# Own input buffers, an early fill and another row order for the last two supertiles of a pointwise convolution

## Chip, cores, metric

One core of a Trainium2 chip. The metric is the device time of one execution in microseconds (us), the median of several runs.

## The reference

```python
# x: (1, 384, 384, 384) bf16, dw: (1, 1, 384), pw: (384, 384)
out = xp[:, i:i+H, j:j+W, :] * dw[i, j]        # k = 1: one scale per channel
return jnp.einsum('bhwc,cd->bhwd', out, pw)
```

With k = 1 this is one matrix product: 147456 rows of 384 channels times a 384 x 384 matrix whose rows are scaled by dw. In and out are 113 MB each.

## The kernel before

Rows go in supertiles of 512, 288 in all. VectorE transposes a supertile, TensorE multiplies it, ScalarE copies the result from PSUM to an output buffer, SyncE issues loads and stores. Loads and stores are made for pieces of 1 to 10 supertiles, in three rotating buffers.

```python
LMAX = 10; NR = 3; LONG = 1
head, tail = [[1, 1, 2, 2, 4]], [[6, 4], [3, 2, 1, 1, 1]]   # between them 26 groups of [10]
...
def load_x(t, eng=nc.sync):
    g, i, off, first, L = chunks[t]
    dst = Xs[g % NR][:, 4 * off : 4 * (off + L), :]
    rows = xf[512 * first : 512 * (first + L), :]
    if first + LONG < NS:                       # all but the last supertile
        src = rows.rearrange("(p s) c -> p (s c)", p=P)        # one run of 3072*L bytes per partition
        ...
    else:                                       # the last supertile
        src = rows.rearrange("(a k q) c -> q a k c", k=4, q=4) # runs of 768 bytes
    ...                                         # waits until the buffer is free
    eng.dma_start(dst, src).then_inc(s_x[g % NR][i], 16)

def store(t):
    ...
    if first + LONG < NS:
        dst = rows.rearrange("(q p j) d -> p q (j d)", q=4, p=P)  # runs of 768*L bytes
    else:
        dst = rows.rearrange("(m q) d -> m (q d)", q=4)           # one run of 3072 bytes
    ...
```

The order of rows within a supertile is free, but the transposes tie input to output. With the plain order the input comes in runs of 3072 bytes and the output leaves in runs of 768; with the other order it is the reverse. Only the last supertile (287) used the other one. Its load was issued by ScalarE, at the copy of supertile 260, late in the run:

```python
for jj, (t, j) in enumerate(order):             # ScalarE's copies, in order
    ...
    a = nc.scalar.copy(Ov[:, 0:nq, j, :], PS[s][:, 0:nq, :D])
    ...
    if jj == g_end[len(groups) - 1 - NR] + 1:   # jj == 260
        for u in range(NT - LONG, NT):
            load_x(u, nc.scalar)
```

Of the kernel before, what the change touches and what calls it, by code (L numbers as in the profile page):

```python
# [7 lines left out]
BF16 = mybir.dt.bfloat16  # L8
F32 = mybir.dt.float32
U32 = mybir.dt.uint32  # L10
# [1 line left out]

LMAX = 10
NR = 3
LONG = 1


def _groups(n_super: int):

    head, tail = [[1, 1, 2, 2, 4]], [[6, 4], [3, 2, 1, 1, 1]]  # L20
    mid = n_super - sum(map(sum, head + tail))
    assert mid > 0 and mid % LMAX == 0
    return head + [[LMAX]] * (mid // LMAX) + tail
# [3 lines left out]
def kernel(  # L27
# [12 lines left out]
    nc = tc.nc  # L40
    P = nc.NUM_PARTITIONS
    B, H, W, C = x.shape
# [8 lines left out]

    NS = N // 512
    groups = _groups(NS)

    chunks, first = [], 0
# [4 lines left out]
    NT = len(chunks)  # L60
    g_end = [max(c[3] + c[4] for c in chunks if c[0] == g) - 1 for g in range(len(groups))]

    consts = ctx.enter_context(tc.tile_pool(name="consts", bufs=1))
    bufp = ctx.enter_context(tc.tile_pool(name="bufs", bufs=1))
# [11 lines left out]
    zero = consts.tile([P, D], BF16, name="zero")  # L76

    Xs = [bufp.tile([P, 4 * LMAX, C], BF16, name=f"X{i}") for i in range(NR)]
    Ts = [bufp.tile([P, NB, 256], BF16, name=f"T{i}") for i in range(2)]
    Os = [bufp.tile([P, 4 * LMAX * D], BF16, name=f"O{i}") for i in range(NR)]  # L80
    PS = [psum.tile([P, 4, 512], F32, name=f"ps{s}") for s in range(2)]

    s_x = [[nc.alloc_semaphore(f"s_x{i}{k}") for k in range(max(map(len, groups[i::NR])))] for i in range(NR)]
    s_t = [[nc.alloc_semaphore(f"s_t{i}{h}") for h in range(2)] for i in range(2)]
    s_pe = nc.alloc_semaphore("s_pe")
    s_a = [nc.alloc_semaphore(f"s_a{i}") for i in range(2)]
# [11 lines left out]
    s_zero = nc.alloc_semaphore("s_zero")  # L98

    with tc.tile_critical():  # L100
        def load_x(t, eng=nc.sync):
            g, i, off, first, L = chunks[t]
            dst = Xs[g % NR][:, 4 * off : 4 * (off + L), :]
            rows = xf[512 * first : 512 * (first + L), :]
            if first + LONG < NS:
                src = rows.rearrange("(p s) c -> p (s c)", p=P)
                dst = dst.rearrange("p s c -> p (s c)")
            else:
                src = rows.rearrange("(a k q) c -> q a k c", k=4, q=4)
            if g >= NR and (i == 0 or eng is not nc.sync):  # L110
                je = g_end[g - NR]
                eng.wait_ge(s_t[je % 2][1], je // 2 + 1)
            eng.dma_start(dst, src).then_inc(s_x[g % NR][i], 16)

        def store(t):
            g, i, off, first, L = chunks[t]
# [2 lines left out]
            rows = of[512 * first : 512 * (first + L), :]  # L119
            if first + LONG < NS:  # L120
                dst = rows.rearrange("(q p j) d -> p q (j d)", q=4, p=P)
# [8 lines left out]

        nc.scalar.dma_start(dw_row[:], dw.rearrange("a e c -> a (e c)")).then_inc(s_dw, 16)
        load_x(0, nc.scalar)
        nc.sync.dma_start(pw_n[:], pw.rearrange("(k p) d -> p k d", p=P)).then_inc(s_pw, 16)

        todo = []
        for t, (g, i, off, first, L) in enumerate(chunks):
            if 0 < t < NT - LONG:
                todo.append((g_end[g - NR] if g >= NR else -1, load_x, t))
            todo.append((first + L + 1, store, t))
# [109 lines left out]
        for s in range(2):  # L249
            c = nc.scalar.copy(warm[:, s + 1 : s + 2], warm[:, 0:1])  # L250
# [4 lines left out]
        def transposes(t, j):  # L255
            g, i, off, first, L = chunks[t]
            jj = first + j
            s = jj % 2
            Xw = Xs[g % NR][:].bitcast(U32)[:, 4 * off : 4 * (off + L), :].rearrange("p (k l) c -> p k l c", l=L)
            Tw = Ts[s][:].bitcast(U32).rearrange("p b (i k) -> p b k i", k=4)  # L260
            for h in range(2):
                if h == 0 and j == 0:
                    nc.vector.wait_ge(s_x[g % NR][i], 16 * sum(len(ls) > i for ls in groups[g % NR : g + 1 : NR]))
                ins = nc.vector.transpose(  # L264
                    out=Tw[:, 3 * h : 3 * h + 3],
                    in_=Xw[:, :, j, 96 * h : 96 * h + 96].rearrange("p k (b w) -> p b k w", w=32),
                )
                if jj >= 2:
                    ins._wait_ge(s_pe, 2 * (jj - 2) + h + 1)
                ins.then_inc(s_t[s][h])  # L270
# [24 lines left out]
        for i in range(6):  # L295
            w_out(i)
        transposes(*order[0])
        transposes(*order[1])

        for jj, (t, j) in enumerate(order):  # L300
            g, i, off, first, L = chunks[t]
            s = jj % 2
            Ov = Os[g % NR][:, 4 * off * D : 4 * (off + L) * D].rearrange("p (q j d) -> p q j d", q=4, d=D)
            if j == 0 and i == 0 and g >= NR:
                nc.scalar.wait_ge(s_o[g % NR], 16 * sum(map(len, groups[g % NR : g : NR])))
            nq = 4
            if jj + 1 == NS:
                nq = 2
                nc.vector.wait_ge(s_o[g % NR], 16 * sum(map(len, groups[g % NR : g : NR])))
                e = nc.vector.tensor_copy(Ov[:, nq:4, j, :], PS[s][:, nq:4, :D])  # L310
                e._wait_ge(s_pe, 2 * jj + 2)
                e.then_inc(s_d)
            a = nc.scalar.copy(Ov[:, 0:nq, j, :], PS[s][:, 0:nq, :D])  # L313
            a._wait_ge(s_pe, 2 * jj + 2)
            a.then_inc(s_a[s])
            if jj == g_end[len(groups) - 1 - NR] + 1:

                for u in range(NT - LONG, NT):
                    load_x(u, nc.scalar)
            if jj + 2 < NS:  # L320
                transposes(*order[jj + 2])

# [29 lines left out]
```

## Time and profile before

| before | |
|---|---|
| time, median of 3 runs | 575.55 us (575.28 to 575.68) |
| the profiled execution | 576.07 us, of which 574.3 us are the span in the profile |
| matmuls of the 288 supertiles | 561.8 us |
| last copy ends, last store issued, landed | 569.63, 569.72, 573.03 us |

The profiled execution was 0.5 us slower than the median.

### The profile page before, as it was taken

Reading aid. Unit: us, or ns where it says so; the run is one execution under the profiler, and the core shown is the slowest. Engines: PE = TensorE matmul, PEld = TensorE weight load, DVE = VectorE, ACT = ScalarE, POOL = GpSimd, SP = SyncE. Lnnn points to the kernel's source line nnn. Section 1 sums busy time; section 2 is a strip of 40 time slices with the busy share of each in tenths; the row PEclk is TensorE's granted clock in tenths of the full one; section 3 lists DMA queues with packets and bytes.
Section 4 is the critical chain, followed back from the end, with each engine's and each line's share of the span. In section 5 each row is a group of like instructions: output and inputs, shape, how many; then the busy total and the mean of one; then the engine's idle time right before and its main releaser. Section 6 shows DMA issues by size and latency. Waiting matters only on the chain.

```text
span 574.3 us, 29720 instructions
## 1 busy us (share of the span) xinstructions
PE 566.5 (99%) x13869; PEld 411.8 (72%) x13869; DVE 509.4 (89%) x583; ACT 418.7 (73%) x296; POOL 0.9 (0%) x8
## 2 busy tenths in 40 slices
PE   8999999999999999999999999999999999999996
PEld 5777777777777777777777777777777777777774
DVE  7899999999999999999999999999999999999994
ACT  6777777777777777777777777777777777777774
POOL 0000000000000000000000000000000000000000
PEclk9999999999999999999999999999999999999999
DMA  8999999999999999999999999999999999999776
GB/s 360 436 376 420 434 409 429 431 431 421 392 399 428 390 385 420 402 388 397 422 402 395 395 439 378 400 394 432 385 402 401 426 399 382 417 400 377 303 280 226
DMA packets 25936, 226.88 MB, mean 395 GB/s; under 512 B 1221, under 2 KB 5702, under 8 KB 22086
## 3 DMA queue, kind: packets, MB, share of 16 engines
q1 hardware_dynamic: 25264, 226.01, 97.6%
q10 hardware_dynamic: 662, 0.79, 0.4%
q14 instruction: 9, 0.07, 0.0%
q8 instruction: 1, 0.02, 0.0%
HBM read 113.54 MB, written 113.25 MB: 395 GB/s over the span
## 4 chain that ended last, share of the span: by engine, by line
PE 98%; ACT 0%; DVE 0%; issue 0%; POOL 0%; POOLq 0%; SPq 0%
PE ps L172 98%; PE ps L189 0%; ACT w_r L277 0%; DVE O L310 0%; PE ps L222 0%; POOL zero L238 0%; POOL warm L237 0%; PE ps L204 0%; POOLq L347 0%; SPq L100 0%
## 5 line engine op out<-in xcount | busy, mean ns | idle before, releaser
L172 PE MATMUL ps<-w_r,T 32*128 32x384 bf16 x13824 | 561.8, 321 | 0.7 <-ACT w_r L277 0.7
L264 DVE STREAM_TRANSPOSE T<-X 128x384 uint32<-128x384 uint32 x576 | 506.3, 881 | 53.7 <-DMA X<-in_x_dram 0.5
L313 ACT CAST O<-ps 128x1536 bf16<-128x1536 f32 x288 | 413.6, 1436 | 147.8 <-PE ps L172 147.8
L172 PEld LDWEIGHTS ps<-w_r,T 32*128 32x128 bf16 x13824 | 410.1, 93 | 152.2 <-issue 0.9
L277 ACT CAST w_r<-ps 128x768 bf16<-128x768 f32 x5 | 3.6, 820 | 1.0 <-PE ps L222 1.0
L189 PE MATMUL ps<-zero 32*128 32x384 bf16 x24 | 2.6, 494 | 1.4 <-POOL zero L238 1.4
L310 DVE CAST O<-ps 128x768 bf16<-128x768 f32 x1 | 1.0, 958 | 3.0 <-PE ps L172 3.0
L250 ACT ACT_TABLE_LOAD x1 | 1.3, 1283 | 1.9 <-issue 1.9
L189 PEld LDWEIGHTS ps<-zero 32*128 32x128 bf16 x24 | 0.7, 99 | 2.6 <-issue 2.6
L222 PE MATMUL ps<-pw_n,sel_w 64*128 64x384 bf16 x18 | 2.2, 395 | 0.0
L282 DVE TENSOR_REDUCE sel<-eye 128x64 f32<-128x128 bf16 x1 | 0.3, 290 | 1.8 <-POOL eye L240 1.8
L222 PEld LDWEIGHTS ps<-pw_n,sel_w 64*128 64x128 bf16 x18 | 0.9, 115 | 1.4 <-issue 0.7
L277 DVE CAST w_r<-ps 128x768 bf16<-128x768 f32 x1 | 1.0, 958 | 0.9 <-PE ps L222 0.9
L292 DVE TENSOR_SCALAR sel_w<-sel,dw_f 128x256 bf16<-128x256 f32 x3 | 0.9, 351 | 0.0
L289 DVE COPY dw_f<-ps 128x3 f32<-128x3 f32 x1 | 0.2, 160 | 0.8 <-PE ps L204 0.8
L204 PEld LDWEIGHTS ps<-ones,dw_row 1*128 1x128 bf16 x3 | 0.2, 102 | 0.2 <-issue 0.2
L240 POOL TENSOR_SCALAR_AFFINE_SELECT eye<-ones 128x128 bf16<-128x128 bf16 x1 | 0.3, 292 | 0.1
L250 ACT COPY warm<-warm 128x1 f32<-128x1 f32 x2 | 0.3, 189 | 0.0
L238 POOL MEMSET zero<- 128x192 uint32 x1 | 0.3, 258 | 0.0
L204 PE MATMUL ps<-ones,dw_row 1*128 1x1 bf16 x3 | 0.2, 162 | 0.0
L239 POOL MEMSET ones<- 128x128 bf16 x1 | 0.2, 204 | 0.0
L336 POOL MEMSET const-bfloat16-1.0<- 128x1 bf16 x1 | 0.1, 102 | 0.0
(4 smaller groups left out, 0.4 us busy)
## 6 DMA issues: line engine op xcount, KB each, us to landing
X<-in_x_dram SPq DMA_DIRECT2D x26, 3840.0 KB, 21.4
out_dram<-O SPq DMA_DIRECT2D x26, 3840.0 KB, 27.6
X<-in_x_dram SPq DMA_DIRECT2D x2, 1536.0 KB, 17.8
out_dram<-O SPq DMA_DIRECT2D x2, 1536.0 KB, 14.5
X<-in_x_dram SPq DMA_DIRECT2D x3, 768.0 KB, 7.1
out_dram<-O SPq DMA_DIRECT2D x3, 768.0 KB, 10.8
X<-in_x_dram SPq DMA_DIRECT2D x1, 2304.0 KB, 20.5
out_dram<-O SPq DMA_DIRECT2D x1, 2304.0 KB, 13.0
```

The lines of the kernel that those rows point to most:

```text
L172: mm = nc.tensor.matmul(PS[s][:, q, :D], lhsT=Ts[s][32 * q : 32 * q + 32, b, par::2], rhs=w_r[32 * q : 32 * q + 32, b, par, :], start=(b, ...
L189: nc.tensor.matmul(PS[0][:, i, :D], lhsT=zero[32 * i : 32 * i + 32, 0:P], rhs=zero[32 * i : 32 * i + 32, :], start=True, stop=True, tile_p ...
L204: mm = nc.tensor.matmul(PS[1][:, 0, D + k : D + k + 1], lhsT=dw_row[:, P * k : P * k + P], rhs=ones[0:1, 0:1], start=True, stop=True,)
L222: mm = nc.tensor.matmul(PS[(k + 1) % 2][:, 2 * r + v, :D], lhsT=sel_w[64 * v : 64 * v + 64, k, r, :, :].rearrange("p q w -> p (q w)"), rhs ...
L238: nc.gpsimd.memset(zero[:].bitcast(U32), 0).then_inc(s_zero)
L240: nc.gpsimd.affine_select(out=eye[:], in_=ones[:], pattern=[[-1, P]], compare_op=mybir.AluOpType.is_equal, fill=0.0, base=0, channel_multi ...
L250: c = nc.scalar.copy(warm[:, s + 1 : s + 2], warm[:, 0:1])
L264: ins = nc.vector.transpose(out=Tw[:, 3 * h : 3 * h + 3], in_=Xw[:, :, j, 96 * h : 96 * h + 96].rearrange("p k (b w) -> p b k w", w=32),)
L277: o = nc.vector.tensor_copy(out, in_) if e == 0 else nc.scalar.copy(out, in_)
L292: nc.vector.tensor_scalar_mul(sel_w[:, k], sel[:].unsqueeze(2).to_broadcast([P, 2, 4, 32]), dw_f[:, k : k + 1]).then_inc(s_sw)
L310: e = nc.vector.tensor_copy(Ov[:, nq:4, j, :], PS[s][:, nq:4, :D])
L313: a = nc.scalar.copy(Ov[:, 0:nq, j, :], PS[s][:, 0:nq, :D])
```

## The change

It means to shorten the end. (Lines with "..." stand for more code.) The last two supertiles (286 and 287) get buffers of their own, so that their loads can be issued long before (at the copies of supertiles 8 and 148), and 286 also gets the row order that stores in runs of 3072 bytes. The pieces of the last eight become 4, 2, 1, 1.

```diff
-LONG = 1
+LONG = 2
+LONG_AT = [8, 148]
-    head, tail = [[1, 1, 2, 2, 4]], [[6, 4], [3, 2, 1, 1, 1]]
+    head, tail = [[1, 1, 2, 2, 4]], [[6, 4], [4, 2, 1, 1]]
+    Xl = bufp.tile([P, 4 * LONG, C], BF16, name="Xl")
+    s_xl = [nc.alloc_semaphore(f"s_xl{n}") for n in range(LONG)]
+        def x_of(t):                # buffer, semaphore and its value for a piece
+            g, i, off, first, L = chunks[t]
+            n = first + LONG - NS
+            if n >= 0:
+                return Xl[:, 4 * n : 4 * n + 4, :], s_xl[n], 16
             ... (else as before)
             if first + LONG < NS:
                 src = rows.rearrange("(p s) c -> p (s c)", p=P)
+                if i == 0 and g >= NR: ... (the wait for the buffer, now here alone)
             else:
                 src = rows.rearrange("(a k q) c -> q a k c", k=4, q=4)
-            if jj == g_end[len(groups) - 1 - NR] + 1:
-                for u in range(NT - LONG, NT):
-                    load_x(u, nc.scalar)
+            if jj in LONG_AT:
+                load_x(NT - LONG + LONG_AT.index(jj), nc.scalar)
```

More of the change, by code (lines that the diff above doesn't have):

```diff
@@ L100 @@
     with tc.tile_critical():
+        def x_of(t):
[3 more added lines that the diff above has]
+                return Xl[:, 4 * n : 4 * n + 4, :], s_xl[n], 16
+            n = sum(len(ls) > i for ls in groups[g % NR : g + 1 : NR])
+            return Xs[g % NR][:, 4 * off : 4 * (off + L), :], s_x[g % NR][i], 16 * n
         def load_x(t, eng=nc.sync):
             g, i, off, first, L = chunks[t]
-            dst = Xs[g % NR][:, 4 * off : 4 * (off + L), :]
+            dst, sem, _ = x_of(t)
             rows = xf[512 * first : 512 * (first + L), :]
@@ L107, in load_x @@
                 dst = dst.rearrange("p s c -> p (s c)")
+                if i == 0 and g >= NR:
+                    je = g_end[g - NR]
+                    eng.wait_ge(s_t[je % 2][1], je // 2 + 1)
             else:
                 src = rows.rearrange("(a k q) c -> q a k c", k=4, q=4)
-            if g >= NR and (i == 0 or eng is not nc.sync):
-                je = g_end[g - NR]
-                eng.wait_ge(s_t[je % 2][1], je // 2 + 1)
-            eng.dma_start(dst, src).then_inc(s_x[g % NR][i], 16)
+            eng.dma_start(dst, src).then_inc(sem, 16)
         def store(t):
@@ L258, in transposes @@
             s = jj % 2
-            Xw = Xs[g % NR][:].bitcast(U32)[:, 4 * off : 4 * (off + L), :].rearrange("p (k l) c -> p k l c", l=L)
+            X, sem, n = x_of(t)
+            Xw = X.bitcast(U32).rearrange("p (k l) c -> p k l c", l=L)
             Tw = Ts[s][:].bitcast(U32).rearrange("p b (i k) -> p b k i", k=4)
@@ L262, in transposes @@
                 if h == 0 and j == 0:
-                    nc.vector.wait_ge(s_x[g % NR][i], 16 * sum(len(ls) > i for ls in groups[g % NR : g + 1 : NR]))
+                    nc.vector.wait_ge(sem, n)
                 ins = nc.vector.transpose(
```

## The prediction

> **What bounds the kernel now.** I read the page first: the busy shares, the chain that ended last, the costliest group.
>
> ```profile
> PE 566.5 (99%) x13869; PEld 411.8 (72%) x13869; DVE 509.4 (89%) x583; ACT 418.7 (73%) x296; POOL 0.9 (0%) x8
> ...
> PE 98%; ACT 0%; DVE 0%; issue 0%; POOL 0%; POOLq 0%; SPq 0%
> ...
> L172 PE MATMUL ps<-w_r,T 32*128 32x384 bf16 x13824 | 561.8, 321 | 0.7 <-ACT w_r L277 0.7
> ```
>
> TensorE spends 561.8 us on the matmuls of 288 supertiles, 1.951 us each, and waited once, 0.7 us, before the first. There is no hole in the middle that better inputs could close. What is not matmul is a head of 6.85 us (the first of these matmuls starts there) and a tail of 574.3 - 568.65 = 5.65 us. The change moves loads and stores only, so it can win in the tail alone, and lose wherever it makes an engine wait. Next, the timeline of the end (start, length, engine, line):
>
> ```profile
> 566.73 1.44 ACT L313 CAST O<-ps 128x1536 bf16<-128x1536 f32 x1 [0.51 <-PE ps L172]
> 568.67 0.80 ACT L313 CAST O<-ps 128x768 bf16<-128x768 f32 x1 [0.51 <-PE ps L172]
> 568.67 0.96 DVE L310 CAST O<-ps 128x768 bf16<-128x768 f32 x1 [3.01 <-PE ps L172]
> ```
>
> The last copy ends at 569.63, SyncE issues the last store at 569.72, and it lands 3.3 us later, at 573.03; 1.3 us of closing steps follow. What fills the 3.3 us? The DMA view of 571.7 to 572.75 us, in 40 slices, answers:
>
> ```profile
> DMA  0020002000020002000020002000200002000000
> GB/s 29 0 117 0 0 0 117 0 0 0 0 117 0 0 0 117 0 0 0 0 117 0 0 0 117 0 0 0 117 0 0 0 0 117 0 0 0 0 0 0
> DMA packets 11, 0.03 MB, mean 24 GB/s; under 512 B 2, under 2 KB 3, under 8 KB 11
> ```
>
> In that last microsecond one packet starts at a time, evenly spaced: a single DMA engine is still working and fifteen have finished. The landing records say the same: the last store's sixteen increments come at 571.88 to 572.03 us (fifteen) and 573.03 us (one). Followed back through all transfers, one increment in sixteen always comes late: by 1.5 us for the first ten-supertile load, some 7 us in the middle, 9 to 10 us at 480 to 540 us, and about 1 us at the end. So one engine is slower and has had work queued since the first loads. Its landings late in the run follow one another by 9.1 us (load of ten) and 10.45 us (store of ten), 19.55 us a group, where TensorE needs 19.51 us. It catches up only when the loads stop. The end is therefore two chains of nearly equal length: TensorE, last copy and last store, which would land at 572.03 us, and the slow engine's backlog, which ends 1.0 us later and sets the time.
>
> **What the Trainium skill says.** "DMA: Bandwidth & Descriptors", section "Why a DMA increments its semaphore by 16 and not by 1": each participating engine posts its own increment after its own data. The trace agrees: 16 recorded increments for nearly every transfer, which is what makes the late engine visible. The same page, "Latency and other measured facts", says that DMA engines 7 and 15 are usually slower; its guess at the cause is for transfers issued from GpSimd, of which there are none here. The trace shows one slow engine of sixteen, not its number. The same page, "Why small descriptors are slow (HBM only)", gives a fixed overhead per packet. The trace agrees on that engine: in the end its 768-byte packets start 33 ns apart, its 3072-byte packets 118 ns. Overhead o and rate r from 33 = o + 768/r and 118 = o + 3072/r: r = 27.1 B/ns, o = 4.7 ns. "Issuing engines are not separate DMA queues": a load from ScalarE runs on the same sixteen engines and saves only issue time, so moving loads to that queue adds no bandwidth. The trace agrees in so far as the ScalarE load issued at 516.03 us drains until 536.6 us beside SyncE's.
>
> **The change part by part.** I count work on the slow engine, which handles 8 of 128 partitions of each transfer.
>
> Stores of the last eight supertiles, before (pieces of 3, 2, 1, 1, 1 supertiles; runs of 2304, 1536, 768, 768, 3072 bytes): 32 packets of 4.7 + 2304/27.1 = 89.7 ns make 2.87 us; 32 of 61.4 ns make 1.96; twice 32 of 33 ns make 2.11; 8 of 118 ns make 0.94. Sum 7.88 us. After (4, 2, 1, 1; runs of 3072, 1536, 3072, 3072): 32 of 118 ns make 3.78; 1.96; twice 0.94 make 1.88. Sum 7.62 us, so 0.26 us saved.
>
> Loads of those supertiles, with the same formula (an estimate, since it was read from stores): before 2.76 + 1.85 + 0.94 + 0.94 for runs of 9216, 6144, 3072, 3072 bytes, and 1.06 for the one with 768, 7.55 us; after 3.67 + 1.85 + twice 1.06, 7.64 us. So 0.09 us is added: the 3072-byte output order of supertile 286 is paid for by a 768-byte input order. Net: -0.17 us on the chain that ends last.
>
> Moving the loads to the evictions of supertiles 8 (24.6 us) and 148 (about 298 us) changes when, not how much. The slow engine has a queue then and later, so its sum is what counts; moving work forward gains nothing. Nobody is starved by it: the second ten-supertile load lands at 34.8 us and is first needed at about 43.6; in mid-run loads land some 16 us before use.
>
> ScalarE pays one more issue. At 516 us an issue took 0.65 us and the next copy started on its beat of 1.95 us (516.02, then 517.98), since it lay under the running copy. Expected cost 0. TensorE's and VectorE's instruction counts do not change, nor do the transposed shapes. The last store is still issued 0.09 us after the last copy.
>
> Sum: 575.55 - 0.17 = 575.4 us.
>
> **Rivals.**
> 1. ScalarE is held at its early issue. SyncE's stores issued from 10 to 36 us show it (durations in ns, min/median/max):
>
> ```profile
> L128 SPq DMA_DIRECT2D out_dram<-O x5: 394/909/13719, 10.6 to 35.0; - x5
> ```
>
> The third store's issue, begun at 16.34 us, took 13.7 us, until 30.06, and the next issues took 2.9, 1.9 and 0.9 us: with two loads of 3840 KB queued, SyncE could not hand over more. ScalarE's new issue comes at 24.63 us, inside this. If the limit is common to both queues, ScalarE is held until 30.1 or even 33 to 35 us. The copy of supertile 9, due at 26.57, would end at 31.6 or later, and TensorE, which needs that buffer at 28.52, would stand still for 3 to 8 us. Minus the 1.0 us that the slow engine's lag absorbs, the time would be 577.5 to 582.5 us. For it: the long issues are real, and the 516 us load's first packet only started at 520.69. Against it: the two queues may have rings of their own, ScalarE's is empty, and the issues of both engines at 1.5 us took 0.37 and 0.47 us side by side. No record shows ScalarE issuing while SyncE is held, so I leave this at 0.3.
> 2. The faster store of 286 gains its full time. Fifteen engines move 384 KB of 768-byte runs at about 330 GB/s and of 3072-byte runs at about 390, 0.2 us apart. But those fifteen stood idle from 570.32 us until the last store's first packet at 570.56, 0.84 us after its issue, so it is hidden there already; only the slow engine feels it, counted above. If the slow engine's whole lag vanished, the floor would be 575.55 - 1.0 = 574.5 us.
> 3. The lag is noise: if that engine's rate drifts by 0.1% of its some 570 us, 0.6 us, the result is anything from 574.9 to 576 us. The three runs of before span 0.4 us.
> 4. The stores of 280 to 283, joined in one, start 1.95 us later than the first part did (562.34 for 560.39). If the slow engine ran dry then, the end would move out. It finishes the previous store only at 564.87, so it does not.
>
> **Range and chances.** Without a hold the result should lie at 574.8 to 575.9 us (0.7); with it at 577.5 to 582.5 (0.3). I give 575.4 as the value, and 574.8 to 579.0 as the range, which takes in the first case and the shorter part of the second. Faster by over 2% (under 564.0) would need more than the whole tail: 0.01. Slower by over 2% (over 587.1) needs a hold of some 13 us or a slow engine starving TensorE: 0.02. Within 2%: 0.97.
>
> **What would show it.** Right: matmul time 561.8 us with no new wait of TensorE; ScalarE's two issues at about 24.6 and 298 us under 1 us long; the copies on their 1.95 us beat; at the end again a single engine working alone for about 0.8 to 0.9 us, and the last store landing about 3.1 us after its issue. Wrong: an issue of ScalarE of several us near 25 us, followed by TensorE waiting for the copy of supertile 9 (then rival 1 holds); or all sixteen increments of the last store together (then the backlog was not conserved, and early loads did relieve the slow engine), with a gain near 1 us.

## More of the kernel before

The waits of SyncE's queue show the end of the program as one number (engine, line, what was waited for: us in total, times, longest us):

```profile
SPq L147 <- DMA out_dram<-O: 3.0, 1, 3.0
```

That is the only wait for a store to land: the last one.

## The result and the profile after

| | median us | range, runs |
|---|---|---|
| before | 575.50 | 575.28 to 576.35, 6 |
| changed | 575.20 | 575.11 to 575.40, 6 |

The ratio is 0.9993, interval 0.998 to 1.0006: same. The value lies in the predicted range, 0.2 us below the predicted 575.4. The matmuls take the same 561.8 us, and no wait of TensorE is new:

```profile
L183 PE MATMUL ps<-w_r,T 32*128 32x384 bf16 x13824 | 561.8, 321 | 0.7 <-ACT w_r L289 0.7
```

First the DMA view of 571.7 to 572.75 us in the changed kernel, the same stretch in which the prediction shows eleven lone packets:

```profile
DMA  0000000000000000000000000000000000000000
GB/s 0 0 0 0 0 0 0 0 0 0 0 0 0 0 0 0 0 0 0 0 0 0 0 0 0 0 0 0 0 0 0 0 0 0 0 0 0 0 0 0
DMA packets 0, 0.00 MB, mean 0 GB/s; under 512 B 0, under 2 KB 0, under 8 KB 0
```

The slow engine is no longer last. The last store is issued at the same 569.72 us, its sixteen increments come at 571.87 to 572.07, and SyncE's wait for it is 1.0 us shorter:

```profile
569.72 0.34 SPq L139 DMA_DIRECT2D out_dram<-O  x1
...
SPq L158 <- DMA out_dram<-O: 2.0, 1, 2.0
```

(Two views, the timeline of SyncE and its waits.) And the first rival of the prediction, that ScalarE is held at its early issue, did not happen. Timeline of ScalarE:

```profile
24.62 1.44 ACT L325 CAST O<-ps 128x1536 bf16<-128x1536 f32 x1 [0.51 <-PE ps L183]
24.63 0.64 ACTq L124 DMA_DIRECT2D Xl<-in_x_dram  x1
26.57 1.44 ACT L325 CAST O<-ps 128x1536 bf16<-128x1536 f32 x1 [0.51 <-PE ps L183]
```

The issue takes 0.64 us while SyncE's own issue is held from 16.34 to 29.84 us, and the next copy starts on its beat. So at this point a full queue of SyncE did not hold ScalarE.

So the profiled span fell by 1.0 us (574.3 to 573.4), the medians by 0.3. The whole lag of the slow engine is gone in this run, where the prediction expected to take 0.17 us off it. The sign that it had named for being wrong, all sixteen increments together, came true. Something in its account of that engine was wrong by a lot.

**A way to read such runs.** In all profiled runs here without a stall of TensorE, the span is a sum of four parts: start to ScalarE's first supertile copy; from there to the last store's issue; that issue to the last landing; closing.

| profiled run | first copy | to last issue | to landing | closing |
|---|---|---|---|---|
| before | 9.03 | 560.69 | 3.31 | 1.32 |
| changed | 9.02 | 560.70 | 2.35 | 1.32 |
| changed, run again (below) | 9.42 | 560.70 | 2.36 | 1.32 |

The second part never moves, the fourth hardly. The third is what this change is about. The first differs from run to run by up to 0.9 us in what follows, with the same code in it. That is why a gain of some tenths is seen in the third part of a trace and not in a median. The third part is not free of chance either, as two_more_early below shows. The same records give the slow engine's place in its work: the time of the sixteenth increment of a transfer, less the time of the first copy.

### The profile page after: what moved, and what is told of

Same layout as the page of the kernel before. It is cut to its first block, busy times and chain, and to the rows that moved or that the text cites. A ratio compares the mean times of both kernels' runs of the same rounds, so it can differ in the third digit from the quotient of the medians.

```text
span 573.4 us, 29717 instructions
## 1 busy us (share of the span) xinstructions
PE 566.5 (99%) x13869; PEld 414.7 (72%) x13869; DVE 506.7 (88%) x583; ACT 419.0 (73%) x296; POOL 0.9 (0%) x8
## 4 chain that ended last, share of the span: by engine, by line
PE 99%; ACT 0%; DVE 0%; issue 0%; POOL 0%; POOLq 0%; SPq 0%
PE ps L183 98%; PE ps L200 0%; ACT w_r L289 0%; DVE O L322 0%; PE ps L233 0%; POOL zero L249 0%; POOL warm L248 0%; PE ps L215 0%; POOLq L358 0%; SPq L103 0%
## 5 line engine op out<-in xcount | busy, mean ns | idle before, releaser
L183 PE MATMUL ps<-w_r,T 32*128 32x384 bf16 x13824 | 561.8, 321 | 0.7 <-ACT w_r L289 0.7
L276 DVE STREAM_TRANSPOSE T<-X 128x384 uint32<-128x384 uint32 x572 | 500.0, 876 | 56.0 <-DMA X<-in_x_dram 0.3
L276 DVE STREAM_TRANSPOSE T<-Xl 128x384 uint32<-128x384 uint32 x4 | 3.5, 876 | 0.4
## 6 DMA issues: line engine op xcount, KB each, us to landing
out_dram<-O SPq DMA_DIRECT2D x1, 2304.0 KB, 11.7
```

Of the source, the lines that this page charges most:

```text
L183: mm = nc.tensor.matmul(PS[s][:, q, :D], lhsT=Ts[s][32 * q : 32 * q + 32, b, par::2], rhs=w_r[32 * q : 32 * q + 32, b, par, :], start=(b, ...
L276: ins = nc.vector.transpose(out=Tw[:, 3 * h : 3 * h + 3], in_=Xw[:, :, j, 96 * h : 96 * h + 96].rearrange("p k (b w) -> p b k w", w=32),)
```

## The experiments

Theory A is the prediction's: the slow engine is always busy, its work is conserved, what counts is its packets. Theory B came from the result: work put early is forgotten, so it is the earliness that emptied the backlog. Theory C arose from the first runs. In what follows "lag" is how far the last store's sixteenth increment comes behind the fifteenth.

**1. Both loads late (label late).**

```diff
-LONG_AT = [8, 148]
+LONG_AT = [260, 261]
```

> The changed kernel with only the times of its two separate loads altered: both issued by ScalarE at the evictions of supertiles 260 and 261 (about 516 and 518 us), as late as the kernel before loads its last supertile. Theory A (the slow DMA engine's work is conserved; what counts is the lengths of the runs, -0.17 us, and not when the loads run): same as the changed kernel, 575.2 us, and the last store's sixteen increments land together. Theory B (the slow engine's queue length late in the run does not remember early work, so it is taking two loads of 0.8 to 1 us each out of the last 60 us that emptied the backlog): the backlog returns, the sixteenth increment of the last store lands 0.5 to 1.2 us after the fifteenth, and the time is 575.5 to 576.2 us, as before.

Measured: 589.07 us (587.48 to 589.94), before 575.41 in the same rounds, ratio 1.0229, interval 1.0213 to 1.0246: slower. Neither theory had that. ScalarE's timeline:

```profile
516.81 0.65 ACTq L124 DMA_DIRECT2D Xl<-in_x_dram  x1
518.75 1.44 ACT L325 CAST O<-ps 128x1536 bf16<-128x1536 f32 x1 [0.51 <-PE ps L183]
518.76 13.79 ACTq L124 DMA_DIRECT2D Xl<-in_x_dram  x1
532.60 1.44 ACT L325 CAST O<-ps 128x1536 bf16<-128x1536 f32 x1 [12.40 <-issue]
```

and who waited for it:

```profile
ACT O L325 <- issue: 12.4, 1, 12.4
PEld ps L183 <- ACT O L325: 11.9, 1, 11.9
PE ps L183 <- ACT O L325: 11.5, 1, 11.5
```

The second issue held ScalarE for 13.8 us, the next copy came 12.4 us late, and TensorE stood for 11.5 us. This is the prediction's first rival, with one part different: what fills up is ScalarE's own queue, from its own earlier load, not SyncE's (in run 3 below, with the other load on SyncE's queue, ScalarE's issue takes 0.65 us). It also says why the change spaces its two loads by 140 supertiles. As a test of A against B by its lag the run is void, since the stall let the slow engine catch up (lag 0.01 us).

**2. Early loads alone (label early_plain).** Buffers and early loads of the change, order and pieces of before.

```diff
+ORDER = 1
-    head, tail = [[1, 1, 2, 2, 4]], [[6, 4], [4, 2, 1, 1]]
+    head, tail = [[1, 1, 2, 2, 4]], [[6, 4], [3, 2, 1, 1, 1]]
-            if first + LONG < NS:          # row order, in load_x and in store
+            if first + ORDER < NS:
```

> The early loads alone: two separate buffers filled at the evictions of supertiles 8 and 148, but supertile 286 in the row order of before (3072-byte runs in, 768-byte runs out) and the pieces of the last eight as before (3, 2, 1, 1, 1). Theory A: no gain, 575.5 us, the sixteenth increment of the last store about 1 us late. Theory B: all of the gain is there, 575.1 to 575.3 us, with the sixteenth increment less than 0.2 us behind the fifteenth.

Measured: 575.28 us (575.13 to 575.54), before 575.41, ratio 0.9997, interval 0.9983 to 1.0011. Lag 0.01 us, 2.33 us from issue to landing. As B expected, against A.

**3. The change's order with late loads (label late_mix).** 286 is loaded by SyncE at 512.0 us, 287 by ScalarE at 516.1 us, so that no two follow each other on ScalarE's queue.

```diff
-LONG_AT = [8, 148]
+LONG_AT = [260]
-            if 0 < t < NT - LONG:
+            if 0 < t < NT - 1:             # SyncE loads 286 too
-                load_x(NT - LONG + LONG_AT.index(jj), nc.scalar)
+                load_x(NT - 1, nc.scalar)
```

> The changed kernel with the earliness alone undone and without two loads following each other on ScalarE's queue: supertile 286 is loaded by SyncE right after the loads of 280 to 285 (about 512 us), 287 by ScalarE at the eviction of supertile 260 (516 us), as in the kernel before; buffers, row order and pieces stay those of the change. Theory A (only the lengths of the runs matter): 575.2 us and the sixteen increments of the last store together. Theory B (the late loads are the backlog): the sixteenth increment 0.5 to 1.1 us behind, 575.4 to 576.0 us, like before. ScalarE's issue stays under 1 us, since it is the only one on its queue.

**4. Half late (label late_one).** `LONG_AT = [8, 260]`.

> Half the dose: 286 early (supertile 8), 287 late (supertile 260), both from ScalarE, all else as in the changed kernel. Theory A: as the changed kernel. Theory B: some 0.8 to 1 us more work late on the slow engine than in the changed kernel, whose slow engine had just caught up at 562.7 us; so the sixteenth increment 0 to 0.6 us behind, 575.1 to 575.6 us. ScalarE's issue at 516 us under 1 us.

Measured: late_mix 575.48 us (575.17 to 575.60), late_one 575.59 us (575.35 to 575.87), before 575.53 in the same rounds, ratios 0.9998 and 0.9999: same. But both have a lag of 0.01 us and 2.36 us from issue to landing:

```profile
569.75 0.34 SPq L139 DMA_DIRECT2D out_dram<-O  x1
...
SPq L158 <- DMA out_dram<-O: 2.0, 1, 2.0
```

(late_mix, SyncE's timeline and waits.) late_one's profiled time is explained by its start, whose first copy came at 9.53 us. So with the order alone, without earliness, there is no backlog at the end either. Theory B as the only cause has fallen too.

What had been missed stood in the landing records. A load in the changed order leaves five landing events, not sixteen: one about 1 us after the issue, and four late ones (the early load at 24.63 us: 25.71, then 42.52 to 42.64, with its packets never more than four at a time). The Trainium skill explains it, in "DMA: Bandwidth & Descriptors", section "Why a DMA increments its semaphore by 16 and not by 1", under "How many engines (k)": the number of engines is the largest number up to 16 that divides the slowest dimension of both sides, and the issuer itself adds the missing increments at once. Here the source pattern is q a k c, its slowest dimension is q = 4, and so such a load runs on **four** engines with 128 packets of 768 bytes each. The trace agrees. **Theory C:** the slow engine is not among the four; the change's row order for 286 takes that load off the slow engine, wherever in time it is put.

**5 and 6. Two useless loads more, early and late (labels two_more_early, two_more_late).** To the kernel before, these add two loads of 384 KB into unused buffers. They were written in the same four-engine order, before Theory C. (A first try, early and late, labels extra_early and extra_late, with four such loads added to the changed kernel, did not build: its buffers leave 0.8 KB per partition.)

```diff
+            if t == EXTRA:                 # piece 12 (about 120 us) or 36 (about 513 us)
+                for u in range(2):
+                    rows = xf[512 * u : 512 * u + 512, :].rearrange("(a k q) c -> q a k c", k=4, q=4)
+                    nc.sync.dma_start(Xe[u][:], rows).then_inc(s_xe, 16)
```

> The kernel before plus two useless loads of 384 KB in 768-byte runs into buffers of their own, issued by SyncE at about 120 us, after a ten-supertile load. They are some 2.1 us of work on the slow engine. Theory A (work conserved on an engine that is always busy): the sixteenth increment of the last store comes 2.5 to 3 us after the fifteenth, 577.3 to 577.8 us. Theory B (early work is forgotten): 575.3 to 575.7 us as before; the slow engine is up to 2 us behind the kernel before at 150 us and under 1 us behind at 500 us.

> The same two useless loads issued by SyncE at about 513 us, after the last loads of the kernel before. Both theories: the slow engine ends 2.1 us later than before, 577.2 to 577.8 us, the sixteenth increment of the last store 2.5 to 3.1 us after the fifteenth. If the time stays at 575.5, the backlog of that engine does not set the end.

Measured: early 575.52 us, before 575.53, same. Late 576.88 us (576.38 to 577.40), ratio 1.0021, interval 1.0008 to 1.0035: clear of noise, 1.35 us longer, less than expected. Knowing the four engines, both expectations had the wrong engine in mind, and early says nothing on A against B. In two_more_late the work fell on four engines, 256 packets each, and some of these were among the last to land (the last store's final increments at 572.84, 573.26 and 573.76 us). Here SyncE was held, too, by the second of the two loads:

```profile
513.60 11.91 SPq L120 DMA_DIRECT2D Xe<-in_x_dram  x2
525.55 7.67 SPq L135 DMA_DIRECT2D out_dram<-O  x1
```

two_more_early has a second thing to teach. Its loads and stores of the last supertiles are those of the kernel before, and yet its last store came with a lag of 0.06 us, 2.42 us after the issue:

```profile
SPq L156 <- DMA out_dram<-O: 2.1, 1, 2.1
```

So the 1.0 us of the one profile of before is not what every run of that code has, and a lag of zero in one profile does not by itself show that a change emptied the backlog. What does is the slow engine's own time for the last loads, which is read below.

**7 to 10. The same, on all sixteen engines.** Each 384 KB load in the changed order is cut into four of 32 partitions, so that the slowest dimension is 32. Applied to late_mix, late and the two useless loads.

```diff
-            eng.dma_start(dst, src).then_inc(sem, 16)             # q a k c, q = 4
+            for q in range(4):                                    # a k c, a = 32
+                eng.dma_start(dst[32 * q : 32 * q + 32], src[q]).then_inc(sem, 16)
```

> The run with late loads in the change's order (286 by SyncE at 512 us, 287 by ScalarE at 516 us), but each of the two loads cut into four of 32 partitions, so that the outermost dimension is 32 and not 4. Theory C: as one transfer such a load runs on four of the sixteen DMA engines (it leaves four late completion increments in the records, not sixteen), none of which is the slow one, so the change took the load of supertile 286 off the slow engine by its order alone. Cut in four, each leaves 4 x 16 increments and loads the slow engine with 2 x 1.06 us again: beside the kernel before, +1.15 us of loads and -0.26 us of stores on it. Expected: the sixteenth increment of the last store 1 to 2 us behind the fifteenth, 576.0 to 576.6 us. Theory B (only the earliness counts, all loads on all engines) has no room for a difference to the uncut run, 575.5 us with no lag.

> The 589 us run (both loads from ScalarE at the evictions of supertiles 260 and 261) with each load cut into four of 32 partitions. Theory C: uncut, a load puts 128 packets into the queues of each of four engines, and the second one holds ScalarE (13.8 us) until the first has drained; cut, it puts 32 into each of sixteen. Expected: no issue of ScalarE above 1.5 us, no wait of TensorE above 1 us, time 576 to 577.5 us, with the slow engine last by 1 to 2.5 us. If ScalarE is held by the number of bytes or of issues, it is held again and the time is 585 us or more.

> The kernel before plus two useless loads at about 120 us, now each cut in four so that they do reach the slow engine: 2.1 us of work on it. Theory A (that engine is always busy and its work is conserved): 577.3 to 577.8 us. Otherwise: 575.3 to 575.7 us, the slow engine about 2 us behind the kernel before near 150 us and less than 0.5 us behind near 500 us.

> The same two useless loads cut in four, at about 513 us. The slow engine gets 2.1 us more at the end: the sixteenth increment of the last store 2.3 to 3.1 us behind, 577.0 to 577.7 us, while the other fifteen are on time (2.2 to 2.4 us after the issue).

Each of the four is "same" by the 2% of the verdicts, with intervals of the ratio that lie above 1 (late_mix_spread 1.0001 to 1.0027, late_spread 1.0102 to 1.0133, more_early_spread 1.0035 to 1.008, more_late_spread 1.0042 to 1.0068). Every one of these cut loads left its 16 increments, so the first part of Theory C, how many engines, is confirmed. The times, before at 575.44 us in the same rounds:

| | median us | range | lag, profiled run |
|---|---|---|---|
| late_mix_spread | 576.33 | 576.05 to 577.07 | 0.01 |
| late_spread | 582.17 | 581.25 to 583.09 | 0.01 |
| more_early_spread | 579.13 | 576.69 to 580.80 | 3.0 |
| more_late_spread | 578.63 | 578.45 to 579.79 | 2.7 |

late_mix_spread hit its range for a reason other than the expected one. The slow engine did get the work (its store of 515 us landed at 543.89 us, in late_mix at 542.07), but ScalarE's four issues took 2.8 us, the copy behind them came late, and with a late start of the run the tail shifted by 1.2 us, in which the slow engine caught up: lag 0.01 us. The expected lag of 1 to 2 us was not seen.

late_spread missed too. No single issue holds ScalarE for long, but from the third on each takes about 1.4 us, two blocks of 4.3 and 5.6 us, and TensorE waits 3.9 us:

```profile
516.34 4.27 ACTq L125 DMA_DIRECT2D Xl<-in_x_dram  x4
520.65 1.44 ACT L328 CAST O<-ps 128x1536 bf16<-128x1536 f32 x1 [2.88 <-PE ps L186]
520.67 5.57 ACTq L125 DMA_DIRECT2D Xl<-in_x_dram  x4
526.28 2.78 ACT L328 CAST O<-ps 128x1536 bf16<-128x1536 f32 x2 [4.18 <-PE ps L186]
```

So cutting eased the hold (6.7 us over before, not 13.7) and did not remove it. That the 13.8 us came from 128 packets in each of four queues is made likely by this, not shown: bytes in flight or the number of issues may count as well.

The two runs with useless loads are the clean ones. Both put 2.1 us (computed) on the slow engine, and TensorE waits for nothing new in either. SyncE's wait for the last store, more_early_spread and then more_late_spread:

```profile
SPq L157 <- DMA out_dram<-O: 5.0, 1, 5.0
```
```profile
SPq L157 <- DMA out_dram<-O: 4.7, 1, 4.7
```

against 3.0 us before. That is 2.0 and 1.7 us more at the end: the backlog of one DMA engine sets the time, and of work put on it at 120 us about as much is still there at 570 us. That is nearer to Theory A's conservation than to B's forgetting. A rival is that SyncE's long issues did it, since in more_early_spread they made the store of 125 us 4.4 us late. two_more_early speaks against it: there the hold was longer (that store 11.7 us late) with no load on the slow engine, and by 457 us that engine was 0.5 us ahead of before. The medians rose by more than that, 3.7 and 3.2 us, and more_early_spread scatters over 4 us; I have no cause for that excess, which the profiled runs (span 2.4 and 2.6 us over that of before) do not fully show. The place of the slow engine in time settles how far conservation goes (us after the first copy, sixteenth increments of the same store in each run, and of the last ten-supertile store in the last line):

```
store issued at   before  changed  early_plain  late_mix  late_one  more_early  more_late
125 us            140.96   142.78     142.25     140.99    142.31     145.34     140.91
223 us            241.05   241.14     241.48     240.57    240.91     244.10     240.93
437 us            457.87   457.31     457.71     456.80    456.86     459.75     456.62
496 us            517.25   516.66     517.04     516.20    516.16     519.26     516.10
515 us            534.80   532.67     533.09     533.02    532.13     537.08     536.70
535 us            545.26   543.09     543.56     543.47    542.60     547.58     547.14
```

Three things are to be read from it. (more_early and more_late are the cut versions; SyncE's issues were held in them, so that the store of 125 us was issued at 129.9 us in more_early and the store of 515 us at 530.35 us in more_late. The columns come from different chips, but the slow engine's pace late in the run is the same in all.)

First, between 140 and 240 us a delayed engine makes up 0.9 to 1.7 us: in before its loads of ten take 9.1 to 9.8 us there, and in a run that is behind they take 9.1. After about 400 us every run does a load in 9.1 us and a store in 10.45, so nothing is made up, and work that arrives then stays. more_early fell 4.4 us behind, twice the computed work, and had 1.9 us left at the store of 437 us, so that 2.0 us come out at the end is in part luck. Work is conserved only in this rough sense, and what is left over at 500 us differs between runs by 1 us for no reason that I can name.

Second, the step from the 496 us store to the 515 us store, in which the last loads lie, is 17.55 us before and 16.01 changed, 16.05 in early_plain, 15.97 in late_one, 16.82 in late_mix, and 20.60 in more_late. Taking the load of 286 out of this stretch, early or onto other engines, is worth 1.5 us there (0.7 in late_mix).

Third, late_one has 287's load of 128 packets on each of four engines in that stretch, 4.2 us by 33 ns a packet, and its step is the shortest: the slow engine is not one of the four. The clearest pair is late and late_spread, which differ in the cut alone: with both loads late on four engines the step is 15.99 us (516.68 to 532.67), cut over sixteen it is 17.77 (515.95 to 533.72). late_mix against late_mix_spread gives 16.82 and 17.87. This is the second part of Theory C. The other runs with 286's load late on all engines have 17.05 us (two_more_early) and 17.81 (more_early), so with 17.55 this step varies by 0.8 us among them, and taking the load out (late_mix apart) gains 1.0 to 1.8 us.

**11 and 12. The last store cut in two, and the changed kernel again (labels split, after_again).**

```diff
-            nc.sync.dma_start(dst, src)                       # supertile 287, runs of 3072 bytes
+            nc.sync.dma_start(dst[:, 2*D:4*D], src[:, 2*D:4*D])    # VectorE's half
+            if jj + 1 == NS:                                       # ScalarE's half, from its own queue
+                nc.scalar.wait_ge(s_a[s], jj // 2 + 2)
+                nc.scalar.dma_start(of[...][:, 0:2*D], Os[...])
```

> The changed kernel with the last store cut in two: ScalarE stores its own half of supertile 287 (runs of 1536 bytes) as soon as its copy ends, SyncE the other half after VectorE's copy. If the tail is now copy, issue and landing alone, with no backlog on the slow engine, each half needs about 0.5 us of packets in place of 0.94 us, and ScalarE's starts 0.16 us sooner: the last landing should come 0.3 to 0.5 us earlier, 1.8 to 2.0 us after SyncE's last issue in place of 2.35, and the time 574.7 to 574.9 us on the median where the changed kernel has 575.2. If the landing is a fixed latency, or a backlog remains, no gain.

> The changed kernel once more, in the same rounds as the run with the cut store, to compare the two and to see whether its gain of 0.3 us over the kernel before repeats: 575.1 to 575.4 us, with the sixteenth increment of the last store within 0.2 us of the fifteenth.

Measured: split 575.26 us (575.09 to 575.93), changed kernel again 575.51 us (575.29 to 575.77), before 575.34 us (575.17 to 576.32); ratios to before 0.9993 (0.9979 to 1.0006) and 0.9997 (0.9984 to 1.0011). All the same. Cutting the store gained nothing: from SyncE's last issue to the last landing it is 2.31 us in place of 2.36. ScalarE's half was issued first:

```profile
569.11 1.82 SPq L141 DMA_DIRECT2D out_dram<-O  x2
...
570.43 0.36 ACTq L334 DMA_DIRECT2D out_dram<-O  x1
```

Its packets started from 571.31 to 571.92 us. SyncE's half was issued at 570.58, yet its first packet started only at 571.83, when the other half was nearly through, and its last at 572.45. Two halves on two queues ran one after the other. The changed kernel again had no lag (2.36 us from issue to landing), but a later first copy (9.42 us) took its gain in time away. No version here beats both kernels clear of noise.

## Why the prediction was right, and where it was not

- **The number.** 575.4 us for 575.20 is in part luck. With the lag gone, the prediction's own floor was 574.5 us, below its range; the range held because a gain of 1.0 us in one pair of profiles is 0.3 us in the medians.
- **What bounds the kernel, and that the time stays.** Right. TensorE's 561.8 us did not move, and the effect in the profiles lies in issue to landing of the last store, 3.31 to 2.35 us. Pooled over all rounds, 44 runs of before reach from 575.17 to 576.97 us, mean 575.60, and 11 of the changed kernel from 575.11 to 575.77, mean 575.35. The pools are not of the same rounds, so this is a hint: the gain is some 0.25 us on average.
- **One slow engine's backlog sets the end.** Right for the profiled run of before, and shown in that work added to it (2.1 us, computed) moved the last landing by 1.7 to 2.0 us, with TensorE undisturbed. Not every run of such code has the lag (two_more_early: 0.06 us).
- **-0.17 us on that engine.** The step that failed reads: "I count work on the slow engine, which handles 8 of 128 partitions of each transfer". For the 768-byte loads that is false. They run on four engines, and the slow one is not among them. So "the 3072-byte output order of supertile 286 is paid for by a 768-byte input order" is false too: the input order costs the slow engine nothing and frees it of a load. In that term's place the trace shows -1.5 us (17.55 to 16.01 us), 0.94 of which is that load by the prediction's own packet times and 0.6 of which stays unexplained, within the 0.8 us by which this step varies in before-like runs. Another 0.6 us was there before the last loads (517.25 to 516.66 at the store of 496 us), and is not shown to come from the change. With the 0.26 us of the stores, which no run tested by itself, this is more than the 1.0 us lag, so the lag went to zero and the rest was idle time of the slow engine.
- **"Moving work forward gains nothing."** Half right. Two early useless loads were still felt at the end. But moving 286's one load early, on sixteen engines, took it out of the last stretch (early_plain: a step of 16.05 us and no lag): between 140 and 440 us that run made up 1.4 us on the kernel before.
- **Rival 1**, ScalarE held by a limit common to both queues: wrong at the early issue (0.64 us while SyncE was held). The same hold by ScalarE's own queue is real, and cost 13.7 us when two loads followed each other.
- **The floor of 574.5 us** was taken from the median less the profiled lag of 1.0 us. The profiled run was itself 0.5 us above the median, so a typical run may have had less to win; two_more_early, without lag, fits this. Profiled against profiled, 576.07 to 575.11 us, the full lag is there. In medians it is 0.3 us once and none the second time.

## What to carry to other kernels

Before you count the work of a transfer per DMA engine, look at the outermost dimension of both its patterns, and in the trace at how many completion increments it leaves: a leading dimension of 4 puts a transfer on four engines, which can hold its issuer and also, as here, spare a slow one. When the end of a program waits for a store, compare its first fifteen increments with the last: if they are together, no backlog of one engine sets it; if one is late, look for that backlog, in more than one profile. Before an engine that computes issues a second DMA while its first still waits in a busy queue, look at the length of such issues: here a second load on four engines held ScalarE for 13.8 us, while four loads of a quarter each took 0.6 to 0.8 us (late_mix_spread), and eight about 1.4 us from the third on (late_spread).

## What the Trainium skill lacked or had wrong

- "DMA: Bandwidth & Descriptors", section "Why a DMA increments its semaphore by 16 and not by 1": its rule for the number of engines held in every load here (5 landing events with an outermost 4, 16 with 32 or 128). It does not add what follows for the issuer. No section of that page says that a queue with too much pending holds the engine that issues: ScalarE was held for 13.8 us by a second load of 512 packets, SyncE for 11.2 us by another, and SyncE for 13.7 us already in the kernel before.
- Same page, section "Latency and other measured facts", on engines 7 and 15: it ties the slowness to GpSimd's transfers. There are none here, and one engine is slower all the same (the trace does not show its number). Alone at 545.9 to 548.2 us it takes 324 to 342 ns for a packet of 7680 bytes, where 12409 of all 13312 such packets took under 300 ns (median 291).
- Same page, section "Queues, rings and completion order", on turns between queues by packet: a load of 128 packets per engine on ScalarE's queue, issued at 297.63 us beside SyncE's traffic, had its first packet at 302 us and its last increment at 366.2 us, 68.6 us after the issue; the one at 24.63 us took 18.0 us. The page gives no hint of such times.
- Same page, section "Issuing engines are not separate DMA queues", says that transfers of several issuers interleave. The two halves of the last store, issued 0.16 us apart on two queues, ran one after the other (packets from 571.31 to 571.92, then from 571.83 to 572.45 us). This is one pair of small transfers; elsewhere two queues did share the time, as with ScalarE's load of 516.03 us in the kernel before, which took from 520.7 to 537.1 us beside SyncE's.
